# Two feed-forward layers after a channel attention: the first layer's cosine taken unreduced in all blocks, with its weights' decoding re-ordered

## The chip, the core and the metric

The program runs on one core of a Trainium2 chip. The metric is the device time of one execution in microseconds (us). Three timed runs of the kernel before gave 997.1, 998.02 and 998.35 us; their median, 998.02 us, is the time that the change is measured against.

## What is computed

With q, k, v of 6016 tokens by 256 channels, q and k are normalised per channel over the tokens, and

```
s = kn.T @ qn / tau            # 256 x 256
a = softmax(s)
x = v @ a                      # 6016 x 256
h = x @ w_in1                  # 256 -> 2048
y = (h * cos(h)) @ w_out1      # 2048 -> 256
out = silu-gated layer 2 of y: (g * sigmoid(g)) @ w_out2 with g = y @ w_in2
```

All four weight matrices come as 64-bit floats and are decoded to 32-bit floats on the core.

## The kernel before

**Stages.** First the q/k tiles are streamed in and the scores s are summed on TensorE; then the softmax; then `a` is folded into w_in1 (a times w_in1), so that the first layer reads v directly; then both layers, with tokens in 12 blocks (eleven of 512, one of 384). TensorE works in 32-bit products split in a high and a low part, three products for one (high*high, low*high, high*low: `PASSES`).

**The stretch that the change touches** runs from the end of the scores to the end of blocks 0, 1 and 2 of the first layer. It is a loop over 24 units (`units`, at the end of `direct`, lines 1103 to 1213). A unit is one block and one pair of 128 hidden columns; units 0 to 15 are blocks 0 and 1 (two units of one, two of the other, in turn), units 16 to 23 block 2. Units 0 to 3 need the first quarter of the folded w_in1, units 4 to 7 the second, and so on. In turn i the loop issues:

- TensorE: `emit_h`, twelve matmuls that make h of unit i in a PSUM room (line 742; two rooms alternate, `next_room`).
- units 0 to 15 only, `emit_first`: ScalarE rounds h/2pi + 1/4 to a whole number (line 749), VectorE subtracts that many times 2pi (line 750). Then `emit_cos`: ScalarE's sine (757) and VectorE's product with h (758), which frees the room. From unit 16 on `cosine_in` (1099) takes the sine of h itself with a scale per block: `small[b]` is 1 where a bound on |h| is at most 1.5 and 0 where it isn't (one 0 makes the program run a general path behind its end).
- `emit_split` of unit i-1: ScalarE writes the high part (763), VectorE the low part (764).
- TensorE: `emit_o1` of unit i-2, twelve matmuls with w_out1 (line 777).

**What rides along.** Strings of short names say what else is issued where; `steps_of` runs them, and each engine works in the order in which things were issued. `BEFORE` comes between softmax and unit 0; `EARLY` has the turns: `ahead` (before h), `amid` (after h), `inner` (after the split), `outer` (after the cosine). For a piece of w_in1 (W) or w_out1 (O), of which there are four each:

- `lW`, `l`: load (SyncE's queue; four raw buffers in a ring).
- `bW`, `bO` (`begin`): ScalarE's absolute value (336), and GpSimd's rounding of the low words (290; `aO`, `aW` put that on ScalarE).
- `cW`, `cO` (`clamp`): VectorE's clamp (295) and shift (303).
- `jW`, `jO` (`join`): VectorE joins sign and word (309), then GpSimd adds the low word (312).
- `sO` (`split`): ScalarE's high part (355), GpSimd's low part (356).
- `f00`, `f01`, `f10`, `f11`, `f2`, `f3` (`fold`): TensorE's matmuls of a quarter or half quarter of w_in1 (672) and ScalarE's high part of it (680). `l00` to `l31` (`fold_low`): VectorE's low part (688). Quarter j of the fold reads piece j of w_in1 after its `jW`.
- `lv`, `s1`, `v1`, `s0`, `v0`: load, high and low part of v's blocks 1 and 0 (401, 452, 455). One raw buffer for v: the next load waits until the last one was read.
- `tb`: a load of ScalarE's table.

`SPANS` places VectorE's maxima of the folded w_in1 (`span_of_weights`, 418); the bounds for blocks 2 and 3 (`bound`, 435 to 440) are made in turns 15 and 22. `FORMING` places work for blocks after these.

Of the kernel before, what the change touches and what calls it, by code (L numbers as in the profile page):

```python
# [53 lines left out]
WARM = (5, 0)  # L54

FRONT = {14: 'lW aW', 15: 'cW', 17: 'jW'}
AFTER = 'lW V l aW lW l cW'
THEN = ['', '', 'lW jW s0', '']
SIDE = [7, 11, 15, 20]
JOINED = 22  # L60
BEFORE = 'aO T0 T1 bW rs f00 v0 cO l00 lv tb f01 l01 cW jO f10 aO l l10'
TURNS = 16
FORMING = {
    12: 'A0', 13: 'A1', 15: 'B0', 16: 'B1', 17: 'V', 18: 'V', 19: 'V A2', 20: 'A3', 21: 'B2', 22: 'B3'
}
# [154 lines left out]
def direct(ctx, tc, qk, vT, tau, w_in1, w_out1, w_in2, w_out2, outT, dp, kept, within):  # L220
# [177 lines left out]
    def load_v(b):  # L398
        t0, n = BLOCKS[b]
        raw = io.tile([P, CH, TB], F32, tag="vraw", name=f"vraw{b}", bufs=1)  # L400
        nc.sync.dma_start(out=raw[:, :, :n], in_=vT.rearrange("(a p) n -> p a n", p=P)[:, :, t0 : t0 + n])
        return raw

    def span_of(b, raw, a=None):
# [9 lines left out]
            apply_absolute_value=True,  # L414
        )

    def span_of_weights(j, a):
        nc.vector.tensor_reduce(
            out=largest[:, j, a : a + 1],
            in_=fold_to(j, a, 0).bitcast(F32),  # L420
            axis=AX.XY,
            op=ALU.max,
            apply_absolute_value=True,
        )
# [16 lines left out]
            out=small[b], in0=most_of_all, scalar1=LIMIT, scalar2=1.0, op0=ALU.is_le, op1=ALU.mult  # L441
        )

    def split_v(b, raw, pool=False):
        n = BLOCKS[b][1]
        hi, lo = xparts[1, b] = [x_tile(s, b) for s in ("hi", "lo")]
        if pool:
            nc.gpsimd.tensor_scalar(
                out=halves(hi[:, :, :n]), in0=turns(raw[:, :, :n]), scalar1=1.0, scalar2=1.0, op0=ALU.mult, op1=ALU.mult
            )  # L450
        else:
            nc.scalar.activation(halves(hi[:, :, :n]), turns(raw[:, :, :n]), AF.Copy)

        def low():
            (nc.gpsimd if pool else nc.vector).tensor_tensor(
                out=halves(lo[:, :, :n]), in0=turns(raw[:, :, :n]), in1=halves(hi[:, :, :n]).bitcast(F32), op=ALU.subtract
            )

        return low
# [36 lines left out]
    calls = {
        "V": lambda: vraw0.append(load_v(0)),
        "s0": lambda: low_v0.append(split_v(0, vraw0.pop())),
        "v0": lambda: low_v0.pop()(),
        "lv": lambda: vraw1.append(load_v(1)),  # L500
        "s1": lambda: low_v1.append(split_v(1, vraw1.pop())),
        "v1": lambda: low_v1.pop()(),
        "p1": lambda: split_v(1, vraw1.pop(), pool=True)(),
        "l": WO1.load,
        "lW": W1.load,
        "bW": W1.begin,
# [151 lines left out]
    def next_room():  # L658
        turn_of[0] += 1
        return ps_hs[(turn_of[0] - 1) % 2]  # L660

    pws = {}

    def fold(j, a):
        if j < 2 or a == 0:
            pool, tag = (ps_o, "o") if j == 1 else (next_room(), "h")
            pw = pool.tile([P, CH, TB], F32, tag=tag, name=f"pw{j}{a}")
            pws.update({(j, i): pw[:, i] for i in ((a,) if j < 2 else range(CH))})
        halves_ = (a,) if j < 2 else range(CH)
        for a in halves_:  # L670
            for d in range(CH):
                nc.tensor.matmul(  # L672
                    pws[j, a],
                    ET[:, d, a * P : (a + 1) * P],
                    w1[:, d, j * TB : (j + 1) * TB],
                    start=(d == 0),
                    stop=(d == CH - 1),
                )
        for a in halves_:
            nc.scalar.activation(  # L680
                fold_to(j, a, 0), pws[j, a].rearrange("p (m f) -> p m f", m=2), AF.Copy, scale=rs[:, a : a + 1]
            )

    def fold_to(j, a, i):
        return wa[j][:, i].rearrange("p m (a f) -> p a m f", a=CH)[:, a]
# [48 lines left out]
    def emit_h(u):  # L734
# [10 lines left out]
    def emit_first(i, u, hp):  # L745
        n = BLOCKS[u[0]][1]
        t = flat(T[i % 2])
        k = t.bitcast(I32)[:, :, :n]
        nc.scalar.activation(k, hp[:, :, :n], AF.Copy, scale=1.0 / TWO_PI, bias=0.25)
        nc.vector.scalar_tensor_tensor(  # L750
            out=t[:, :, :n], in0=k, scalar=-TWO_PI, in1=hp[:, :, :n], op0=ALU.mult, op1=ALU.add
        )
        return t

    def emit_cos(u, hp, t):
        n = BLOCKS[u[0]][1]
        nc.scalar.activation(t[:, :, :n], t[:, :, :n], AF.Sin, bias=half_pi)
        nc.vector.tensor_tensor(out=t[:, :, :n], in0=hp[:, :, :n], in1=t[:, :, :n], op=ALU.mult)
# [349 lines left out]
    vs = []  # L1108
    for i, u in enumerate(units):
        b, m = u  # L1110
        steps_of(EARLY["ahead"].get(i, ""))
        if i == TURNS - 1:
            pro.close()
            rp = ctx.enter_context(tc.tile_pool(name="rp", bufs=1))
# [8 lines left out]
        if bounded is not None:  # L1123
            emit_o1(units[i - LAG], parts[i - LAG], (0,))
            if bounded == FIRST:
                ready.append(h_tile(f"bound{bounded}"))
                bound(bounded, ready[0][:, 1])
            else:
                bound(bounded, o1_room(bounded)[:, 0])
# [6 lines left out]
        if i < TURNS:  # L1136
            emit_cos(u, hp, t)
        else:
            cosine_in(b, hp, flat(T[i % 2]))
        pend = i  # L1140
        steps_of(EARLY["outer"].get(i, ""))
        if i >= TURNS:
# [296 lines left out]
    def tail_of_first(j):  # L1439
        nonlocal q_sums, late  # L1440
        _, b, m = slots[j]
        aside(b, m)
        behind(b, m)
        if m == 2:
            load_x2(0)
        if m == 4:
            p1_room.close()
            sp = ctx.enter_context(tc.tile_pool(name="sp", bufs=1, side="right"))
            q_sums = sp.tile([P, NU, HB], F32, name="q")
            late = [sp.tile([P, NU, HB], F32R, name=f"late{k}") for k in range(2)]  # L1450
            nc.vector.tensor_reduce(out=every, in_=smalls[:, FIRST:], axis=AX.X, op=ALU.min)
# [153 lines left out]
```

## Time and profile before

| | |
|---|---|
| median of three runs | 998.02 us (997.1 to 998.35) |
| the profiled execution | 998.62 us, of which its span (first to last instruction) is 996.8 us |
| TensorE busy | 983.0 us, 99% of the span |
| VectorE, ScalarE, GpSimd busy | 839.8, 792.9, 402.6 us |
| granted TensorE clock | 0.999 of full speed over the span |

The busy time of TensorE is from matmuls whose ends are modelled, so a small wait can hide in it; how far TensorE gets is better read from the start times of its groups of twelve matmuls. Times in the rows are us from the span's start; PE is TensorE, PEld its weight load, DVE VectorE, ACT ScalarE, POOL GpSimd, SPq SyncE's queue, L764 line 764.

### The profile page before, as it was taken

How to read it: one execution, taken by the hardware profiler on the slowest of the kernel's cores; microseconds unless marked ns; L12 is line 12 of the kernel's file. 1: busy time of each engine (PE TensorE's matmuls, PEld its weight loads, DVE VectorE, ACT ScalarE, POOL GpSimd, SP SyncE). 2: the span in 40 equal slices, each digit the busy share in tenths (PEclk: the TensorE clock that was granted, in tenths of full speed). 3: DMA queues.
4: the chain of work that ended last, by engine and by line, in shares of the span. 5: the costliest groups of instructions: out<-in, count | busy, mean ns of one | idle time of the engine just before them, and what ended most of it. 6: DMA issues, size and time to landing. Idle time of an engine off the chain costs nothing.

```text
span 996.8 us, 18691 instructions
## 1 busy us (share of the span) xinstructions
PE 983.0 (99%) x7062; PEld 927.6 (93%) x7062; DVE 839.8 (84%) x1287; ACT 792.9 (80%) x1453; POOL 402.6 (40%) x383
## 2 busy tenths in 40 slices
PE   9999999999999999999999999999999999999997
PEld 8867888899999999999999999999999999999997
DVE  5789898988878787888874889999999999999972
ACT  6786667688888888888876888888888888888863
POOL 4443277848678677686463111111111111111100
PEclk9999999999999999999999999999999999999999
DMA  9931005813434333334479722022022022121001
GB/s 339 382 125 51 1 4 240 321 59 127 159 127 159 138 127 137 138 133 149 179 278 383 308 104 84 25 85 72 36 85 75 33 86 67 41 86 49 33 12 40
DMA packets 35011, 126.58 MB, mean 127 GB/s; under 512 B 3170, under 2 KB 4450, under 8 KB 30178
## 3 DMA queue, kind: packets, MB, share of 16 engines
q1 hardware_dynamic: 34770, 125.12, 34.1%
q8 instruction: 57, 0.93, 0.4%
q14 instruction: 40, 0.33, 0.1%
q10 hardware_dynamic: 144, 0.20, 0.1%
HBM read 73.01 MB, written 52.30 MB: 126 GB/s over the span
## 4 chain that ended last, share of the span: by engine, by line
PE 87%; DVE 7%; ACT 2%; issue 2%; DMA 2%; POOL 0%; SPq 0%; DVEq 0%; ACTq 0%
PE o L991 20%; PE xz L991 20%; PE o L1343 16%; PE ys L991 15%; PE o L777 5%; PE h L742 3%; PE o L1031 2%; DMA qk<-qk_dram 2%; PE S L547 1%; DVE lo L764 1%; PE pw L672 1%; PE xz L1020 1%; PE ys L1020 1%; PE xz L1298 1%; PE ys L1298 1%
## 5 line engine op out<-in xcount | busy, mean ns | idle before, releaser
L807 DVE TENSOR_TENSOR lo<-t,hi 128x768 fp32r<-128x768 f32 (+1 forms) x176 | 194.9, 1117 | 28.9 <-ACT hi L799 28.8
L794 POOL TENSOR_TENSOR t<-t 128x256 f32<-128x256 f32 x88 | 64.4, 732 | 356.8 <-DVE t L791 296.8
L799 ACT ACTIVATE hi<-t 128x768 fp32r<-128x768 f32 (+1 forms) x176 | 168.9, 960 | 27.0 <-PE o L991 26.4
L1343 PE MATMUL o<-hi,wo 128*128 128x512 f32 x512 | 142.0, 380 | 0.0
L991 PE MATMUL o<-hi,wo 128*128 128x256 f32 x770 | 134.7, 275 | 0.0
L991 PEld LDWEIGHTS o<-hi,wo 128*128 128x128 f32 x770 | 117.1, 192 | 0.0
L991 PE MATMUL o<-lo,wo 128*128 128x256 f32 x385 | 105.9, 275 | 0.0
L1343 PEld LDWEIGHTS o<-hi,wo 128*128 128x128 f32 x512 | 87.4, 191 | 6.8
L1397 DVE TENSOR_TENSOR xz<-xz,t 128x512 f32<-128x512 f32 x64 | 44.7, 698 | 41.1 <-ACT t L1391 40.1
L1343 PE MATMUL o<-lo,wo 128*128 128x512 f32 x256 | 76.2, 380 | 0.0
L991 PEld LDWEIGHTS ys<-xhi,wf 128*128 128x128 f32 x384 | 67.8, 190 | 8.1 <-DVE ys L1041 1.0
L991 PE MATMUL ys<-xhi,wf 128*128 128x256 f32 x384 | 74.3, 275 | 1.0 <-DVE ys L1041 0.8
L991 PEld LDWEIGHTS o<-lo,wo 128*128 128x128 f32 x385 | 74.0, 192 | 0.0
L991 PE MATMUL xz<-xhi,wa 128*128 128x256 f32 x384 | 71.9, 276 | 0.0
L1501 ACT ACTIVATE ys<-xz 128x256 f32<-128x256 f32 x88 | 32.4, 368 | 45.8 <-PE xz L991 44.8
L991 PEld LDWEIGHTS xz<-xhi,wa 128*128 128x128 f32 x384 | 62.9, 191 | 3.4
L991 PE MATMUL xz<-x2hi,wf 128*128 128x256 f32 x352 | 65.8, 275 | 0.0
L991 PE MATMUL xz<-x2hi,wa 128*128 128x256 f32 x352 | 65.8, 275 | 0.0
L777 PE MATMUL o<-hi,wo 128*128 128x512 f32 (+1 forms) x256 | 62.5, 367 | 0.0
L786 DVE TENSOR_TENSOR t<-t 128x512 f32<-128x512 f32 x88 | 60.3, 685 | 0.1
L1531 ACT ACTIVATE t<-t 128x512 f32<-128x512 f32 x88 | 55.6, 632 | 2.3 <-DVE t L1041 2.1
L1388 ACT ACTIVATE ys<-xz 128x256 f32<-128x256 f32 x64 | 23.6, 368 | 38.9 <-PE xz L991 38.9
(268 smaller groups left out, 3186.7 us busy)
## 6 DMA issues: line engine op xcount, KB each, us to landing
qk<-qk_dram SPq DMA_DIRECT2D x22, 512.0 KB, 7.6
x2hi<-xshi SPq DMA_DIRECT2D x11, 896.0 KB, 5.3
x2lo<-xslo SPq DMA_DIRECT2D x11, 896.0 KB, 7.1
wi_dram<-stage SPq DMA_DIRECT2D x8, 1024.0 KB, 3.9
wo_dram<-stage SPq DMA_DIRECT2D x8, 1024.0 KB, 4.1
vraw<-vT_dram SPq DMA_DIRECT2D x11, 512.0 KB, 4.0
outT_dram<-q SPq DMA_DIRECT2D x22, 256.0 KB, 2.0
xshi<-t SPq DMA_DIRECT2D x10, 512.0 KB, 5.3
```

The costliest lines, as they stand in the source:

```text
L742: nc.tensor.matmul(hp[:, s, :n], lhsT, rhs, start=(i == 0), stop=(i == len(todo) - 1))
L777: nc.tensor.matmul(o[:, e, :n], wo1_at(i, f)[:, e * P : (e + 1) * P], columns(parts[k][:, s, :n]), start=(f == 0 and (i, k) == PASSES[0]), ...
L786: eng.tensor_tensor(out=t[:, 4:6, :c], in0=t[:, 0:1, :c].to_broadcast([P, 2, c]), in1=t[:, 1:3, :c], op=ALU.subtract)
L794: eng.tensor_tensor(out=t[:, 7, :c], in0=t[:, 3, :c], in1=t[:, 6, :c], op=ALU.subtract)
L799: nc.scalar.activation(hi[:, sl, :c], t[:, 1:][:, sl, :c], AF.Copy)
L807: nc.vector.tensor_tensor(out=lo[:, sl, :c], in0=t[:, 1:][:, sl, :c], in1=hi[:, sl, :c].bitcast(F32), op=ALU.subtract)
L991: nc.tensor.matmul(out, w(p, ka), columns(x[r][:, kb - 1]), start=(start and i == 0), stop=(stop and i == 2), skip_group_check=True,)
L1343: nc.tensor.matmul(o[:, e], wo1_at(i, f)[:, e * P : (e + 1) * P], columns(parts[k][:, s]), start=(f == 0 and (i, k) == PASSES[0]), stop=(f ...
L1388: nc.scalar.activation(y2, x2, AF.Copy)
L1397: nc.vector.tensor_tensor(out=xz[k], in0=xz[k], in1=sines[:, 1], op=ALU.mult)
L1501: nc.scalar.activation(y2, x2, AF.Copy)
L1531: nc.scalar.activation(t[:, 0:2], t[:, 0:2], AF.Silu)
```

## The change

Units 0 to 15 take their cosine as block 2 does: `emit_first` and `emit_cos` go, `cosine_in` is called for all 24. Its scale for blocks 0 and 1 comes from a bound per block and quarter of w_in1 (`bound_piece`): two small matmuls of the quarter's column maxima (`largest`) with the maxima of the block (`firsts`), a maximum and a comparison on VectorE, and the sine waits for that comparison. For the first quarter this is done in turn 0 (block 0) and turn 2 (block 1), for the others in turns 4, 8 and 12 for both blocks at once; there the bound's matmuls stand between the two halves of `emit_o1`.

The order of what rides along is new. w_out1's piece 0, not w_in1's piece 1, is decoded during the scores. Only the first quarter is folded before unit 0. Fold 1 stands in turn 3, fold 2 in turn 6 and fold 3 in turn 10, each between the turn's h and its o (`amid`); their high parts (`e1`, `e2`, `e3`), low parts and maxima (`w10`, `w11`, ...) follow in `outer`. w_in1's piece 2 is clamped and joined in the `outer` of turn 5, piece 3 clamped in that of turn 8 and joined in that of turn 9. Block 0's low part (`v0`) goes from VectorE to GpSimd; `x0` and `x1` are VectorE's maxima of blocks 0 and 1.

```diff
-AFTER = 'lW V l aW lW l cW'
-THEN = ['', '', 'lW jW s0', '']
+AFTER = 'l V lW aO l lW cO'
+THEN = ['', '', 'jO s0', '']
-BEFORE = 'aO T0 T1 bW rs f00 v0 cO l00 lv tb f01 l01 cW jO f10 aO l l10'
+BEFORE = 'v0 sO T0 T1 bW rs f00 x0 lv l00 f01 w00 l01 w01 tb x1 s1 l'
-SPANS = {1: (0, 0), 3: (0, 1), 5: (1, 0), 7: (1, 1), 9: (2, 0), 11: (2, 1), 12: (3, 0), 13: (3, 1)}
-EARLY = {'ahead': {2: 'f11', 3: 'cO', 6: 'f2 l21 l20', 10: 'f3 l31 l30'}, 'amid': {3: 'bW'}, 'inner': {0: 's1 v1', 1: 'jW', 2: 'l11', 6: 'cO', 11: 'jO'}, 'outer': {0: 'sO', 3: 'jO', 4: 'sO', 5: 'cW jW bO', 7: 'jO', 9: 'l sO bO', 10: 'cO', 12: 'sO'}}
+EARLY = {
+    'amid': {3: 'f1', 6: 'f2', 10: 'f3'},
+    'mid': {0: 'v1'},
+    'outer': {
+        0: 'cW', 1: 'bO jW', 2: 'cO lW', 3: 'e1 l10 l11 bW w10 w11', 4: 'jO', 5: 'cW jW sO l',
+        6: 'e2 l20 l21 bO w20 w21', 7: 'cO jO bW', 8: 'cW sO', 9: 'jW',
+        10: 'e3 l30 l31 bO w30 w31', 11: 'cO jO', 12: 'sO',
+    },
+}
...
+    def bound_piece(j, bs, room):
+        n = len(bs)
+        to, most_of_all = room[:, : n * TB // P], room[:, P : P + n]
+        for a in range(CH):
+            nc.tensor.matmul(
+                to,
+                largest[:, j, a : a + 1].to_broadcast([P, P]),
+                firsts[:, a, bs[0] : bs[-1] + 1].rearrange("p b j -> p (b j)"),
...
+        nc.vector.tensor_reduce(out=most_of_all, in_=to.rearrange("p (b j) -> p b j", b=n), axis=AX.X, op=ALU.max)
+        nc.vector.tensor_scalar(
...
+        "v0": lambda: low_v.pop(0)(nc.gpsimd),
+        "x0": lambda: span_of_first(0, raw_v.pop(0)),
+        "x1": lambda: span_of_first(1, raw_v[1]),
...
+    def cosine_in(i, h):
+        b, m = units[i]
+        out = flat(T[i % 2])
+        j = m // 2 * FIRST + b
+        nc.scalar.activation(out, h, AF.Sin, bias=half_pi, scale=smalls[:, j : j + 1] if b < FIRST else small[b])
+        steps_of(EARLY["mid"].get(i, ""))
         nc.vector.tensor_tensor(out=out, in0=h, in1=out, op=ALU.mult)
...
         hp = emit_h(u)
-        bounded = {TURNS - 1: FIRST, TURNS + 6: FIRST + 1}.get(i)
+        bounded = i in (4, 8, 12, TURNS - 1, TURNS + 6)
+        if bounded:
             emit_o1(units[i - LAG], parts[i - LAG], (0,))
-        if i < TURNS:
-            t = emit_first(i, u, hp)
+        if i in (0, 2):
+            bound_piece(0, (b,), o1_room(b)[:, 0])
         steps_of(EARLY["amid"].get(i, ""))
         if pend is not None:
             parts[pend] = emit_split(pend, units[pend])
-        steps_of(EARLY["inner"].get(i, ""))
+        if i == TURNS + 6:
+            bound(FIRST + 1, o1_room(FIRST + 1)[:, 0])
+        elif bounded:
+            ready.append(h_tile(f"bound{i}"))
+            if i < TURNS - 1:
+                bound_piece(i // 4, range(FIRST), ready[0][:, 1])
+            else:
+                bound(FIRST, ready[0][:, 1])
+        cosine_in(i, hp)
         pend = i
         steps_of(EARLY["outer"].get(i, ""))
```

At the end of the kernel the smallest of all the comparisons, now 18 columns and not 10, decides on the fallback.

## Rows read from the trace of the kernel before

**Rows 1.** The page: busy time of each engine, its share of the span, instructions.
```profile
PE 983.0 (99%) x7062; PEld 927.6 (93%) x7062; DVE 839.8 (84%) x1287; ACT 792.9 (80%) x1453; POOL 402.6 (40%) x383
```

**Rows 2.** TensorE's waits, 45 to 200 us: us in total, times, longest.
```profile
PE o L777 <- DVE lo L764: 1.7, 3, 0.9
...
PE h L742 <- DVE t L758: 1.2, 1, 1.2
...
PE bound L742 <- DVE smalls L440: 0.6, 1, 0.6
```

**Rows 3.** The last chain in order of time, 80 to 148 us: start, us, what.
```profile
88.45 3.43 PE pw L672 x8
91.88 2.59 PE h L742 x12
```

**Rows 4.** TensorE's timeline: first fold, h of unit 4, o of units 8, 14.
```profile
51.28 5.32 PE L672 MATMUL pw<-w,ET 128*128 128x512 f32 x12
...
76.63 1.10 PE L742 MATMUL h<-xhi,wa 128*128 128x512 f32 x4
...
118.54 1.03 PE L777 MATMUL o<-hi,wo 128*128 128x512 f32 x4
...
150.63 1.03 PE L777 MATMUL o<-hi,wo 128*128 128x512 f32 x4
```

**Rows 5.** Groups, 51 to 190 us: busy us, mean ns | idle before, releaser.
```profile
L750 DVE SCALAR_TENSOR_TENSOR t<-t,h 128x1024 f32<-128x1024 int32 x16 | 19.5, 1220 | 2.2 <-ACT t L749 2.1
L758 DVE TENSOR_TENSOR t<-h,t 128x1024 f32<-128x1024 f32 x16 | 19.5, 1217 | 0.4
...
L749 ACT ACTIVATE t<-h 128x1024 int32<-128x1024 f32 x16 | 16.4, 1025 | 12.5 <-PE h L742 10.3 <-DVE lo L764 2.1
...
L1100 ACT ACTIVATE t<-h,half_pi,smalls 128x1024 f32<-128x1024 f32 x6 | 7.2, 1200 | 1.1 <-PE h L742 1.1
...
L688 DVE SCALAR_TENSOR_TENSOR wa<-pw,rs,wa 128x512 fp32r<-128x512 f32 x8 | 5.8, 749 | 2.8 <-ACT wa L680 2.8
...
L680 ACT ACTIVATE wa<-pw,rs 128x512 fp32r<-128x512 f32 x8 | 5.1, 677 | 0.9 <-PE pw L672 0.9
...
L290 POOL TENSOR_SCALAR raw_wo<-raw_wo 128x1024 int32<-128x1024 uint32 x2 | 3.2, 1604 | 0.2
```

**Rows 6.** VectorE's and GpSimd's timelines, 91 to 95 us: a decode.
```profile
91.29 0.68 DVE L295 TENSOR_SCALAR w<-w 128x1024 f32<-128x1024 f32 x1
92.00 0.69 DVE L303 TENSOR_SCALAR w<-w 128x1024 int32<-128x1024 int32 x1
92.73 1.50 DVE L309 SCALAR_TENSOR_TENSOR w<-raw_w,w 128x1024 int32<-128x1024 int32 x1
94.15 0.67 DVE L418 TENSOR_REDUCE largest<-wa 128x1 f32<-128x512 f32 x1
...
94.31 2.43 POOL L312 TENSOR_TENSOR w<-w,raw_w 128x1024 int32<-128x1024 int32 x1 [5.16 <-DVE w L309]
```

**Rows 7.** VectorE's and GpSimd's timelines, 136 to 142 and 173 to 177 us.
```profile
136.47 2.04 DVE L764 TENSOR_TENSOR lo<-t,hi 128x1024 fp32r<-128x1024 f32 x1
...
139.57 1.21 DVE L409 TENSOR_REDUCE most<-vraw 128x8 bf16<-128x1024 f32 x1
...
136.15 3.50 POOL L957 TENSOR_TENSOR w1base<-wa 128x512 f32<-128x512 f32 x2
139.73 1.43 POOL L965 TENSOR_TENSOR w1form<-w1base 128x256 f32<-128x256 f32 x2
...
173.00 1.21 DVE L862 TENSOR_TENSOR t<-y,t 128x1024 fp32r<-128x1024 f32 x1
...
173.16 3.32 POOL L965 TENSOR_TENSOR w1form<-w1base 128x256 f32<-128x256 f32 x2 [0.63 <-DVE w1base L957]
```

**Rows 8.** VectorE's maximum for a bound; landing of v's block 1, issued at 53 us.
```profile
147.47 0.16 DVE L439 TENSOR_REDUCE bound<-bound 128x1 f32<-128x4 f32 x1
...
DMA to landing us min/median/max: 4.0/4.0/4.0
```

More of the change, by code (lines that the diff above doesn't have):

```diff
@@ L48 @@
 GROUPS = [1, 1] + 22 * [2] + [1]
+FIRST = 2
 LATE = 4
@@ L248, in direct @@
     most = {}
-    largest = wp.tile([P, 4, CH], F32, name="largest")
+    largest = wp.tile([P, 4, CH], BF16, name="largest")
     widest = wp.tile([P, CH], BF16, name="widest")
     every = wp.tile([P, 1], F32, name="every")
-    smalls = wp.tile([P, NB], F32, name="smalls")
-    small = {b: smalls[:, b : b + 1] for b in range(NB)}
+    smalls = wp.tile([P, 4 * FIRST + NB - FIRST], F32, name="smalls")
+    small = {b: smalls[:, 3 * FIRST + b : 3 * FIRST + b + 1] for b in range(FIRST, NB)}
+    firsts = wp.tile([P, CH, FIRST, TB // P], BF16, name="firsts")
     class Weights:
@@ L415, in span_of, with span_of_first @@
         )
+    def span_of_first(b, raw):
+        nc.vector.tensor_reduce(
+            out=firsts[:, :, b],
+            in_=raw.rearrange("p a (j n) -> p a j n", n=P),
+            axis=AX.X,
+            op=ALU.max,
+            apply_absolute_value=True,
+        )
+    def bound_piece(j, bs, room):
[6 more added lines that the diff above has]
+                firsts[:, a, bs[0] : bs[-1] + 1].rearrange("p b j -> p (b j)"),
+                start=(a == 0),
+                stop=(a == CH - 1),
+            )
+        nc.vector.tensor_reduce(out=most_of_all, in_=to.rearrange("p (b j) -> p b j", b=n), axis=AX.X, op=ALU.max)
+        nc.vector.tensor_scalar(
+            out=smalls[:, FIRST * j + bs[0] : FIRST * j + bs[-1] + 1],
+            in0=most_of_all,
+            scalar1=LIMIT,
+            scalar2=1.0,
+            op0=ALU.is_le,
+            op1=ALU.mult,
+        )
     def span_of_weights(j, a):
@@ L442, in bound, with split_v, low @@
         )
-    def split_v(b, raw, pool=False):
+    def split_v(b, raw):
         n = BLOCKS[b][1]
         hi, lo = xparts[1, b] = [x_tile(s, b) for s in ("hi", "lo")]
[L447 to L455, printed above, removed]
+        nc.scalar.activation(halves(hi[:, :, :n]), turns(raw[:, :, :n]), AF.Copy)
+        def low(eng=nc.vector):
+            eng.tensor_tensor(
                 out=halves(lo[:, :, :n]), in0=turns(raw[:, :, :n]), in1=halves(hi[:, :, :n]).bitcast(F32), op=ALU.subtract
@@ L493, in direct @@
     )
-    vraw0, vraw1, low_v0, low_v1 = [], [], [], []
+    raw_v, low_v = {}, {}
     calls = {
[L497 to L503, printed above, removed]
+        "V": lambda: raw_v.update({0: load_v(0)}),
+        "s0": lambda: low_v.update({0: split_v(0, raw_v[0])}),
+        "v0": lambda: low_v.pop(0)(nc.gpsimd),
+        "x0": lambda: span_of_first(0, raw_v.pop(0)),
+        "lv": lambda: raw_v.update({1: load_v(1)}),
+        "x1": lambda: span_of_first(1, raw_v[1]),
+        "s1": lambda: low_v.update({1: split_v(1, raw_v.pop(1))}),
+        "v1": lambda: low_v.pop(1)(),
         "l": WO1.load,
@@ L662, in direct, with fold_room, fold_high, fold_half @@
     pws = {}
+    def fold_room(j, halves_):
+        pw = next_room().tile([P, CH, TB], F32, tag="h", name=f"pw{j}{halves_[0]}")
+        pws.update({(j, i): pw[:, i] for i in halves_})
     def fold(j, a):
[L665 to L681, printed above, removed]
-            )
+        for d in range(CH):
+            nc.tensor.matmul(
+                pws[j, a],
+                ET[:, d, a * P : (a + 1) * P],
+                w1[:, d, j * TB : (j + 1) * TB],
+                start=(d == 0),
+                stop=(d == CH - 1),
+            )
+    def fold_high(j, a):
+        nc.scalar.activation(
+            fold_to(j, a, 0), pws[j, a].rearrange("p (m f) -> p m f", m=2), AF.Copy, scale=rs[:, a : a + 1]
+        )
+    def fold_half(a):
+        fold_room(0, (a,))
+        fold(0, a)
+        fold_high(0, a)
+    def fold_whole(j):
+        fold_room(j, range(CH))
+        for a in range(CH):
+            fold(j, a)
+    def fold_highs(j):
+        for a in range(CH):
+            fold_high(j, a)
     def fold_to(j, a, i):
@@ L697, in direct @@
     for j in range(NF // 4):
-        calls[f"f{j}"] = lambda j=j: fold(j, 0)
+        calls[f"f{j}"] = lambda j=j: fold_whole(j)
+        calls[f"e{j}"] = lambda j=j: fold_highs(j)
         for a in range(CH):
-            calls[f"f{j}{a}"] = lambda j=j, a=a: fold(j, a)
+            calls[f"f0{a}"] = lambda a=a: fold_half(a)
             calls[f"l{j}{a}"] = lambda j=j, a=a: fold_low(j, a)
+            calls[f"w{j}{a}"] = lambda j=j, a=a: span_of_weights(j, a)
     steps_of(BEFORE)
@@ L743, in emit_h @@
         return hp
[L745 to L758, printed above, removed]
     def emit_split(i, u):
@@ L1110, in direct @@
         b, m = u
-        steps_of(EARLY["ahead"].get(i, ""))
         if i == TURNS - 1:
@@ L1121, in direct @@
         hp = emit_h(u)
-        bounded = {TURNS - 1: FIRST, TURNS + 6: FIRST + 1}.get(i)
-        if bounded is not None:
+        bounded = i in (4, 8, 12, TURNS - 1, TURNS + 6)
+        if bounded:
             emit_o1(units[i - LAG], parts[i - LAG], (0,))
[L1125 to L1129, printed above, removed]
-        if i < TURNS:
-            t = emit_first(i, u, hp)
+        if i in (0, 2):
+            bound_piece(0, (b,), o1_room(b)[:, 0])
         steps_of(EARLY["amid"].get(i, ""))
@@ L1134, in direct @@
             parts[pend] = emit_split(pend, units[pend])
-        steps_of(EARLY["inner"].get(i, ""))
[L1136 to L1139, printed above, removed]
+        if i == TURNS + 6:
[7 more added lines that the diff above has]
+        cosine_in(i, hp)
         pend = i
@@ L1155, in direct @@
             vraw = load_v(FIRST + 1)
-        if i in SPANS:
-            span_of_weights(*SPANS[i])
         for what in FORMING.get(i, "").split():
@@ L1173, in direct @@
             v = units[i - LAG]
-            emit_o1(v, parts.pop(i - LAG), (0, 1) if bounded is None else (1,))
+            emit_o1(v, parts.pop(i - LAG), (1,) if bounded else (0, 1))
             if v[1] == NPAIR - 1:
@@ L1450, in tail_of_first @@
             late = [sp.tile([P, NU, HB], F32R, name=f"late{k}") for k in range(2)]
-            nc.vector.tensor_reduce(out=every, in_=smalls[:, FIRST:], axis=AX.X, op=ALU.min)
+            nc.vector.tensor_reduce(out=every, in_=smalls, axis=AX.X, op=ALU.min)
             nc.vector.tensor_copy(within, every[0:1])
```

3 lines of the change are left out of this document (removed).

## Prediction

> **What bounds the kernel now.** The busy row comes first: TensorE is busy 99% of the span, the next engine 84% [rows 1]. A wait of TensorE is therefore lost for good, and work taken off another engine counts only where TensorE waits for it. So the second view is who waited for whom in the stretch that is changed: three waits for a low part (1.7 us), one of h for its room (1.2 us), one for a bound (0.6 us) [rows 2]. The third is the chain, for the price of TensorE's own work: 2.59 us for twelve matmuls of h or o, 3.43 us for a whole fold [rows 3]. With these prices TensorE's start times tell what is lost [rows 4]. From h of unit 4 (76.63) to o of unit 8 (118.54) are 41.9 us; thirteen groups and two folds are 13 x 2.59 + 2 x 3.43 = 40.5; lost: 1.4. From there to o of unit 14 (150.63) are 32.1 us for twelve groups, 31.1; lost: 1.0. More than what is lost up to here and before unit 4 can't be won.
>
> The fourth view is the one that decides: VectorE's and GpSimd's operations side by side. A low part (two inputs in SBUF) takes 2.04 us beside GpSimd's operations, while a like operation before which nothing runs takes 1.21 [rows 7]. The pair of GpSimd's operations at 136.15 ends at 139.65, and 3.50 is just 1.2 + 1.1 + 1.2: one of GpSimd's, the low part, the other one. At 173 GpSimd was released by VectorE, but VectorE's next operation had begun 0.16 us earlier and took its plain 1.21; GpSimd's pair took 3.32 where it takes 1.43 alone [rows 7]. So **these operations run one after the other, each whole**, and at a hand-over VectorE's next one is first: it starts a little before the last one ends (94.15 against 92.73 + 1.50), GpSimd's add at 94.31 [rows 6]. A reduction with one input keeps 1.21 beside GpSimd [rows 7], and so does the product, which reads PSUM.
>
> **What goes.** ScalarE's rounding, 16 of 1.03 us, and VectorE's subtraction, 16 of 1.22 us [rows 5]. Both lie beside TensorE's 5.2 us per unit; the waits for a low part and a room are what they cost. I take all of those waits from unit 4 to unit 14 as gone.
>
> **What comes, up to unit 4.** I take 1.2 for the sine [rows 5], 1.14 for a product or low part (1.22 less the 0.08 that neighbours overlap), and start to start 0.7 for clamp and for shift, 1.42 for the sign step, 2.4 for GpSimd's add [rows 6]. A bound costs TensorE between 0 and two full matmuls (2.59 / 6 = 0.43); its two have a few columns, so I take 0.1. Its maximum and comparison take 0.4 with their hand-overs [rows 8].
> - From 51.28: two half folds to 54.7; the second half's high part 0.7 to 55.4 and low part 0.75 to 56.15 [rows 5]; nine of h's twelve matmuls remain: 58.1. Bound to 58.6, sine 59.8, product 61.0. TensorE ends h of unit 1 at 60.8, so h of unit 2 waits 0.2 for its room. The two maxima x0, x1 (1.21 each, like the row at 139.57) fit before the bound; x1 is queued ahead of the bound's maximum and waits for block 1, which if it lands 4.0 after 53.4 [rows 8] costs 0.4 more; fewer loads are ahead of it now, so I take 0.
> - From 61.0 VectorE does clamp, shift, low part 0, product 1 (to 64.7), the sign step of w_in1's piece 1 (66.1) and block 1's bound (66.5). GpSimd's add came first meanwhile and holds low part 1 back to 68.6; that ends at 69.7, product 2 at 70.85. Fold 1 needs the room that product 2 frees, and TensorE is there at 61.0 + 3 x 2.59 + 0.1 = 68.9: it **waits 1.95**. After fold and o, h of unit 4 starts at 76.9, against 76.63: +0.3.
>
> Three moves I cost at 0. v0 on GpSimd (2.4) lies beside both half folds and the wait for their high parts; without that cover its overrun would show. The loads moved on SyncE's queue have three turns and more (over 15 us) to their decode, with nothing urgent behind them; one that is late costs at most its landing, some 4 [rows 8]. The swapped pieces have the same size, so softmax starts as before.
>
> **Fold 2.** Zero is the end of h of unit 4. Half of o 1.3, bound 1.4, compared 1.8, sine 3.0, product 4.15, sign step of w_out1's piece 1 (turn 4) 5.6, low part 4 first, 6.7; GpSimd's add runs 6.7 to 9.1; product 5 at 7.85. Now turn 5's clamp of w_in1's piece 2 stands in VectorE's queue: does it wait for the add? No row shows a clamp beside GpSimd. From below: it doesn't (0.7, like the one-input reduction); from above: it waits for all of GpSimd's operation. I take the upper value: at 0.68 us for 1024 columns [rows 6] it reads as fast as an operation with two inputs, twice as fast as the reduction. So clamp 9.8, shift 10.5, sign step 11.95, low part 5 first 13.1, add 15.5. Fold 2 reads that piece, and TensorE is there at 5.3 (h of unit 5) + 2.59 + 2.59 = 10.5: it **waits 5.0**. Behind it stands o of unit 4, and everything after.
>
> The Trainium skill, page "SBUF — State Buffer", section "Who interferes with whom", says that a tensor_scalar can run in a mode that uses both of VectorE's port pairs, and then VectorE and GpSimd exclude each other for a whole instruction. No run shows this yet for clamp and shift; by it the total below stands, without it the first rival's does.
>
> **Fold 3.** Zero is the end of h of unit 8. Product 7 was at -2.85; clamp, shift and sign step of w_out1's piece 2 to 0, low part 7 to 1.15, GpSimd's add to 3.55, its rounding of w_in1's piece 3 (1.6 [rows 5]) to 5.15. Product 8 is at 4.15, the clamp of piece 3 waits to 5.15 and ends at 5.85; GpSimd's low part of w_out1 (2.4, as the add) to 8.25; shift 9.0, low part 8 10.1, product 9 11.25, sign step 12.7, low part 9 13.8, add 16.2. TensorE is there at 10.5: it **waits 5.7**.
>
> **Sum.** To unit 4: +0.3. To o of unit 8: +5.0 + 5.7 + 0.2 (two bounds) - 1.4 = +9.5. To o of unit 14: 1.0 lost before, 0.2 now (two bounds): -0.8. Behind that the order is the same, and TensorE hides the rest: 0. Together +9.0. The profiled execution took 998.62 us, its span 996.8 and 1.8 around it; +9.0 gives 1007.6. It was 0.6 above the median of 998.02, so the forecast for the median is **1007.0 us**.
>
> **The rivals.**
> - *Clamp and shift don't wait for GpSimd.* Fold 2: clamp and shift to 9.3, add done at 14.25, wait 3.75. Fold 3: low part 8 waits for GpSimd's to 7.55, add done at 14.8, wait 4.3. That is 2.65 less: 1004.4. For it: no row shows the opposite. Chance 0.20.
> - *GpSimd's add is first after the sign step.* It would end 1.1 earlier in both folds: 1004.7; with the first rival too 1002.1. The row at 173.16 speaks against it. Chance 0.15.
> - *Nothing waits for the other engine.* Then fold 1 doesn't wait (-1.95), fold 2 waits 2.6 (add done at 13.1), fold 3 1.2: 998.2, no change. The row of 2.04 us speaks against it; for it, that GpSimd is free for long stretches. Chance 0.10.
> - *The decode is done before the fold asks*, and the relief of VectorE remains: no fold waits, so 9.0 - 1.95 - 5.0 - 5.7 = -3.65: 994.4, faster. It decides from the point where the add is done within 5.2 us of the end of the h before (that of unit 5, of unit 9); with the two waits under 1.6 us together the kernel is faster by over 2 us. Against it: sine, product, sign step and add alone are 1.2 + 1.14 + 1.42 + 2.4 = 6.2. Chance 0.05.
> - That the bounds fail and the general path runs too is no case of its own: those of blocks 2 to 11 take maxima over all quarters, these over one.
>
> **How the numbers follow.** The forecast has 0.50. The range goes from 1002.0, where the first two rivals meet, to 1009.5: block 1 landing late 0.4, and up to half a microsecond for VectorE being late at each of the four bounds from turn 4 on. Below lie the last two rivals with 0.15. A measurement of this kernel tells about 0.2%, 2 us, from no change. All cases but the last two are slower by more: 0.85; within: 0.10; faster: 0.05.
>
> **What would show it.** In the profile after, TensorE's waits should name fold 2 and fold 3 (line of the fold's matmuls) behind GpSimd's add of w_in1, about 5 us each, and fold 1 behind the product, about 2. GpSimd's add should show 3.5 us behind a sign step, and the clamp of piece 2 and shift of piece 3 well over 0.7. The three waits for low parts between units 4 and 14 should be gone. If the folds start within a microsecond of the end of the h before them, I am wrong; if they wait 2.6 and 1.2, it is the exclusion that isn't there.

## The result and the profile after

The changed kernel takes **1011.7 us** (median of 4 runs, 1010.8 to 1012.5) against 998.1 for the kernel before (997.1 to 998.4, now with a fourth run): ratio 1.014, 95% interval 1.012 to 1.0155. It is slower by 13.6 us where 9.0 were forecast; 1011.7 lies above the range (1002.0 to 1009.5). The profiled execution took 1012.3 us, its span 1010.4, so 13.6 more span than the 996.8 of before.

The busy row, which answers to [rows 1]:
```profile
PE 987.2 (98%) x7072; PEld 929.4 (92%) x7072; DVE 826.5 (82%) x1282; ACT 778.0 (77%) x1435; POOL 412.4 (41%) x386
```
VectorE is busy 13.3 us less and ScalarE 14.9 less, as the change set out to do. But TensorE is busy 4.2 us *more* (983.0 before), though it got only a few tiny matmuls for the bounds. A matmul that is busy for longer without more work is the first sign of the part that the prediction didn't have.

TensorE's waits, 45 to 210 us (total, times, longest), which answer to [rows 2]:
```profile
PE pw L705 <- POOL w L321: 9.7, 2, 5.1
PE pw L705 <- DVE t L1140: 1.7, 1, 1.7
...
PE h L792 <- DVE t L1140: 1.1, 1, 1.1
PE o L812 <- DVE lo L799: 0.8, 1, 0.8
```
Two folds (line 705) wait 9.7 us together for GpSimd's add of w_in1 (line 321); fold 1 waits for a product. No wait for a low part is left up to o of unit 14; the one of 0.8 us stands at 207 us. TensorE's timeline, which answers to [rows 4], shows where and how long each is:
```profile
50.91 3.60 PE L705 MATMUL pw<-w,ET 128*128 128x512 f32 x8
...
62.24 1.10 PE L792 MATMUL h<-xhi,wa 128*128 128x512 f32 x4 [1.15 <-DVE t L1140]
...
72.05 3.67 PE L705 MATMUL pw<-w,ET 128*128 128x512 f32 x8 [1.65 <-DVE t L1140]
...
96.02 6.47 PE L705 MATMUL pw<-w,ET 128*128 128x512 f32 x8 [4.61 <-POOL w L321]
...
128.49 5.60 PE L705 MATMUL pw<-w,ET 128*128 128x512 f32 x8 [5.13 <-POOL w L321]
...
165.30 1.03 PE L812 MATMUL o<-hi,wo 128*128 128x512 f32 x4
```
Folds 2 and 3 wait 4.61 and 5.13 us, and then the same eight matmuls take 6.47 and 5.60 us, where the chain of before has a fold at 3.43 [rows 3] and fold 1 here has 3.67. That is 3.04 + 2.17 = **5.2 us that stand in no wait**. The table of stretches tells where most of them come from: the row holds the stretch, its length, busy us of TensorE, its weight loads, VectorE, ScalarE and GpSimd, then the granted clock.
```profile
91.20:96.00 4.80, 0.21 (x1) 0.00 (x0) 3.62 (x4) 1.97 (x2) 3.27 (x2) 0.87 0.91 318
96.00:98.00 2.00, 1.98 (x3) 0.95 (x4) 0.00 (x0) 0.00 (x0) 2.00 (x1) 0.50 0.04 14
98.00:100.00 2.00, 2.00 (x4) 0.90 (x3) 0.00 (x0) 0.00 (x0) 1.43 (x2) 0.50 0.00 0
100.00:102.00 2.00, 2.00 (x5) 0.78 (x3) 0.00 (x0) 0.00 (x0) 0.00 (x0) 0.60 0.00 0
102.00:104.00 2.00, 2.00 (x10) 1.57 (x9) 0.18 (x1) 1.48 (x3) 0.00 (x0) 1.00 0.00 0
```
During this wait the granted clock begins to fall (0.87 over the whole wait), and through most of the fold it is 0.50, the lower of its two levels (1.2 GHz): three to five matmuls in 2 us, where from 102 us on, at 2.4 GHz again, there are ten. Fold 3 shows the same (0.50 from 128.4 to 132). So these two folds ran most of their length at half speed; fold 1, which had waited 1.65 us, ran at full speed.

The chain of waits from fold 1's end to fold 2 (start, us, what), which answers to [rows 3]:
```profile
82.28 0.18 DVE bound L446
...
82.76 1.22 ACT t L1138
...
85.14 1.50 DVE wv_wo L318
86.64 1.13 DVE lo L799
87.77 1.14 DVE t L1140
88.91 1.70 DVE w L304
90.63 0.70 DVE w L312
...
91.36 1.24 DVE w L318
...
92.73 3.24 POOL w L321
...
96.02 6.47 PE pw L705 x8
```
This is the queue of the prediction, piece by piece: bound, sine, product, sign step of w_out1, low part 4, product 5, clamp, shift, sign step, add. VectorE and GpSimd side by side, which answers to [rows 6]:
```profile
88.83 1.77 DVE L304 TENSOR_SCALAR w<-w 128x1024 f32<-128x1024 f32 x1
...
92.50 1.22 DVE L799 TENSOR_TENSOR lo<-t,hi 128x1024 fp32r<-128x1024 f32 x1
```
```profile
86.79 3.24 POOL L321 TENSOR_TENSOR wv_wo<-wv_wo,raw_wo 128x1024 int32<-128x1024 int32 x1 [15.06 <-DVE wv_wo L318]
92.73 3.23 POOL L321 TENSOR_TENSOR w<-w,raw_w 128x1024 int32<-128x1024 int32 x1 [2.69 <-DVE w L318]
```
The clamp, 0.68 us alone [rows 6], takes 1.77: it ends 0.57 us after GpSimd's first add does (90.03), which is about its own length. The add takes 3.2 us instead of 2.43, since low part 5 began 0.23 us ahead of it. Ahead of fold 3 the shift of piece 3 shows the same against GpSimd's low part of w_out1:
```profile
118.74 2.78 DVE L312 TENSOR_SCALAR w<-w 128x1024 int32<-128x1024 int32 x1
```

The account in stretches, as the lead of the kernel before. At h of unit 4 it is 1.5 us (78.14 against 76.63). O of unit 8 is read from the chain of both profiles, since in the timeline the modelled end of the slow fold overlaps it; the first row is after, the second before:
```profile
134.08 2.59 PE o L812 x12
```
```profile
118.70 2.59 PE o L777 x12
```
That is a lead of 15.4, 13.9 more: 9.7 of waits and 5.2 of slow folds, less 1.1 for the relief net of the bounds. At o of unit 14 it is 14.7 (165.30 against 150.63), 0.7 less. Behind that it shrinks by another 1.1, to 13.6.

### The profile page after: what moved, and what is told of

It reads as the page before. It is cut to its first block, busy times and chain, and to the rows that moved or that the text cites. A ratio compares the mean times of both kernels' runs of the same rounds, so it can differ in the third digit from the quotient of the medians.

```text
span 1010.4 us, 18715 instructions
## 1 busy us (share of the span) xinstructions
PE 987.2 (98%) x7072; PEld 929.4 (92%) x7072; DVE 826.5 (82%) x1282; ACT 778.0 (77%) x1435; POOL 412.4 (41%) x386
## 4 chain that ended last, share of the span: by engine, by line
PE 83%; DVE 8%; POOL 3%; issue 2%; DMA 2%; ACT 1%; SPq 0%; DVEq 0%; POOLq 0%; ACTq 0%
PE o L1026 20%; PE xz L1026 20%; PE o L1377 16%; PE ys L1026 15%; PE o L812 3%; DVE lo L799 2%; PE pw L705 2%; PE o L1066 2%; DMA qk<-qk_dram 2%; DVE t L1140 1%; PE S L582 1%; PE h L792 1%; POOL w1form L1000 1%; PE xz L1055 1%; PE ys L1055 1%
## 5 line engine op out<-in xcount | busy, mean ns | idle before, releaser
L1535 ACT ACTIVATE ys<-xz 128x256 f32<-128x256 f32 x88 | 32.4, 368 | 45.8 <-PE xz L1026 44.8
L1026 PE MATMUL o<-hi,late 128*128 128x256 f32 x308 | 53.8, 275 | 0.0
```

Source lines behind the costliest of these rows:

```text
L1026: nc.tensor.matmul(out, w(p, ka), columns(x[r][:, kb - 1]), start=(start and i == 0), stop=(stop and i == 2), skip_group_check=True,)
L1535: nc.scalar.activation(y2, x2, AF.Copy)
```

## The experiments

The ratios are to the kernel before, timed on the same chip. Differences to the changed kernel's 1011.7 us are between medians of a few runs from different sessions, between which the kernel before moved by 0.8 us (997.4 to 998.2).

**The clock by itself.** Ahead of folds 2 and 3 TensorE gets matmuls to do whose result is overwritten by the fold:
```
 def fold_whole(j):
     fold_room(j, range(CH))
+    for _ in range({2: 20, 3: 23}.get(j, 0)):
+        nc.tensor.matmul(
+            pws[j, 0], wo1_at(0, 0)[:, :P], wo1[0][:, 0, 0, :TB], start=True, stop=True, skip_group_check=True
+        )
     for a in range(CH):
         fold(j, a)
```


> The changed kernel with idle matmuls put ahead of folds 2 and 3 (20 and 23 products of 128x128 by 128x512, whose result the fold overwrites), so that TensorE works through its two waits. Theory (the waits of 4.6 and 5.1 us let the granted clock fall, and the folds behind them run at half of it): both folds take 3.4 us again, not 6.5 and 5.6, the granted clock stays at 1.0, and the time falls by 3.0 + 2.2 = 5.2, to about 1006.5 us; the folds still start when GpSimd's add is done. Rival (the folds are slow for what they read, a piece that GpSimd has just written): folds as slow as before, 1011.7 us or more.

Measured: 1008.5 us, ratio 1.011 (1.010 to 1.013), span 1006.8. The folds took 3.70 and 3.59 us and the clock stayed at 1.00 through both waits and both folds; the rival, which blames what the folds read, falls. The time is 2.0 above the 1006.5 that was expected. Part of that is that the 23 matmuls ahead of fold 3 held it until 126.38, 0.7 us beyond the end of the decode (125.69). So 20 in both places were tried:

> The run that filled the waits ahead of folds 2 and 3 with idle matmuls, with 20 instead of 23 of them ahead of fold 3, since the 23 ran 0.75 us beyond the decode's end. Theory (the clock's fall behind a wait costs 5.2 us, of which the first such run got back 4.4 and lost 0.75 to its own excess): both folds at 3.4 to 3.8 us, fold 3 starts within 0.2 us of its data, and the time is 0.5 to 0.8 us below that run's 1008.5, 1007.7 to 1008.1, ratio to the kernel before 1.0097 to 1.0105. Rival (with fewer of them the clock falls again ahead of fold 3): fold 3 takes over 5 us and the time is over 1009.

Measured: 1007.7 us, ratio 1.0096 (1.0081 to 1.0112); the profiled execution took 1007.1. TensorE's timeline of this run:
```profile
90.52 4.73 PE L726 MATMUL pw<-wo 128*128 128x512 f32 x20
95.34 3.70 PE L705 MATMUL pw<-w,ET 128*128 128x512 f32 x8
120.38 4.83 PE L726 MATMUL pw<-wo 128*128 128x512 f32 x20 [0.47 <-DVE t L1144]
125.10 3.70 PE L705 MATMUL pw<-w,ET 128*128 128x512 f32 x8
```
The decode is no faster, and the folds start when it ends, as before; only TensorE is kept at work. That alone gives back 4.0 us of the median and 5.2 of the span, of which 1.0 is the first fold's earlier start (49.92 against 50.91). The two folds are 2.77 + 1.90 = 4.7 us shorter. So of the 5.2 us above 4.7 are the clock's, a cost of its own on top of the wait; the other 0.5 is that a fold which starts afresh takes 3.70 at the upper clock too, where one that follows at once on other matmuls adds 3.43.

**Who is first at the hand-over.** Two tiny reductions (two columns, their result is overwritten later) go behind the sign steps of w_in1's pieces 2 and 3: VectorE gets more to do, but its next operation after the sign step is now a reduction with one input, of the kind that kept its time beside GpSimd [rows 7].
```
-4: 'jO', 5: 'cW jW sO l',
+4: 'jO', 5: 'cW jW z sO l',
...
-8: 'cW sO', 9: 'jW',
+8: 'cW sO', 9: 'jW z',
...
+for _ in range(2):
+    nc.vector.tensor_reduce(out=every, in_=smalls[:, :2], axis=AX.X, op=ALU.min)
```


> The changed kernel with work added to VectorE: two tiny one-input reductions (0.2 us each) behind the sign steps of w_in1's pieces 2 and 3, in turns 5 and 9. Theory (VectorE and GpSimd exclude each other, and VectorE's next operation is first at a hand-over): with a reduction next, GpSimd's add starts at once, takes 2.4 and not 3.2 to 3.4 us, the low part behind it waits instead; the folds wait about 0.8 to 1.1 us less each, so 1009.5 to 1010 us, and less if the clock falls later for it. Rival (GpSimd's add is slow by itself or for memory traffic): the add stays at 3.2 to 3.4, the time at 1011.7 or up to 0.8 above.

Measured: 1008.7 us, ratio 1.011 (1.010 to 1.013): more work for VectorE, and less time (3.0 us in the median, 1.7 between the two profiled executions). VectorE's and GpSimd's timelines behind the sign step:
```profile
92.58 0.34 DVE L554 TENSOR_REDUCE every<-smalls 128x1 f32<-128x2 f32 x2
92.85 3.43 DVE L805 TENSOR_TENSOR lo<-t,hi 128x1024 fp32r<-128x1024 f32 x1
...
92.81 2.37 POOL L321 TENSOR_TENSOR w<-w,raw_w 128x1024 int32<-128x1024 int32 x1 [2.69 <-DVE every L554]
```
GpSimd's add begins 0.04 us ahead of the low part, and now it is the low part that takes 3.43 us and the add that takes its plain 2.37. The waits fell by 0.86 and 0.98, to 3.75 and 4.15; the folds still took 5.40 and 6.22 (granted clock 0.50 in the midst of both), so most of the clock's part stayed.

**Where in the queue the decode stands.** One run brings w_in1's piece 3 ahead of w_out1's piece in turns 8 and 9 (the second pair of lines below); a second run has this and does the same for piece 2 in turns 4 and 5 (both pairs):
```
-4: 'jO', 5: 'cW jW sO l',
+4: 'cW jW', 5: 'jO sO l',
...
-8: 'cW sO', 9: 'jW',
+8: 'cW jW', 9: 'sO',
```


> The changed kernel with only piece 3 of w_in1 joined earlier (turn 8 in place of 9, and w_out1's split in turn 9). Theory: fold 3's wait falls from 5.1 to under 1 us and its fold from 5.6 to 3.4; fold 2 stays at a wait of 4.6 and 6.5 us for the fold: -4.4 - 2.2 = -6.6, about 1005 us. Rival (the second wait follows from the first, whatever the order): fold 3 still waits over 3 us.

Measured: 1005.7 us, ratio 1.009 (1.007 to 1.011). Fold 3 waits 1.09 and takes 3.70; fold 2, untouched, waits 4.58 and takes 5.40.

> The changed kernel with the decode of w_in1's pieces 2 and 3 a turn earlier and ahead of w_out1's: clamp and join of piece 2 in turn 4 (w_out1's join from turn 4 to turn 5), clamp and join of piece 3 in turn 8 (w_out1's split from turn 8 to turn 9). Theory (the folds wait because their piece is joined in the turn just before): fold 2 doesn't wait, fold 3 under 1 us; o of unit 4 now waits some 3 to 4 us for w_out1's low part, which is late in place of it; no wait is long enough to bring the clock down for a whole fold. -4.6 - 5.1 - 5.2 + 3.7 + 0.7 = -10.5: about 1001 us. Rival (the folds wait for their PSUM room or for VectorE's lateness in general): both waits stay, within 2 us of 1011.7.

Measured: 1002.3 us, ratio 1.0056 (1.0035 to 1.0077). Fold 2 waits 0.19, fold 3 1.14, both take 3.70. Now o of unit 4 waits 1.77 for w_out1's low part, which was put behind. Both runs add up to within the noise. In the first, fold 3 loses 4.0 us of wait and 1.9 of slow clock, and the untouched fold 2 happens to take 1.1 less than in the changed kernel: 7.0 together, against 6.8 in the spans of the profiled executions (1003.6 against 1010.4) and 6.0 in the medians. In the second, fold 2 loses 4.4 and 1.7, and 2.7 come back (o of unit 4 waits 0.94 for w_out1's high part, too): 3.4 together, against 2.8 in the spans and 3.4 in the medians. Executions of one and the same kernel spread over 3 to 4 us here.

**The bounds.** The five bounds of blocks 0 and 1 go; ones stand as the scale, so the condition under which the unreduced cosine may be taken is left out for these blocks.

> The changed kernel without the five bounds of blocks 0 and 1 (their scale is a column of ones; the comparison that they stand for is left out). Theory (the place of the decode makes the waits, the bounds only lengthen the chain ahead of them): fold 1 waits 0.9 and not 1.65, fold 2 about 1.5 less than 4.6, fold 3 about as long as now; 1.0 for the bounds' matmuls and fold 1, 1.5 for fold 2: about 1009 us, some 2 less if the clock falls less in fold 2. Rival (it is the sine's wait for a bound that holds the folds up): both long waits go, 1000 us or less.

Measured: 1008.6 us, ratio 1.011 (1.009 to 1.012), near the 1009 that were forecast. Without the bounds (their maxima are still taken) folds 2 and 3 still wait, so the rival falls; the bounds are worth about 3 us of the 13.6. The rows of TensorE's timeline hold something else:
```profile
94.34 3.70 PE L706 MATMUL pw<-w,ET 128*128 128x512 f32 x8 [3.63 <-POOL w L321]
...
123.84 6.76 PE L706 MATMUL pw<-w,ET 128*128 128x512 f32 x8 [5.07 <-POOL w L321]
```
After 3.63 us of waiting the fold ran at the upper level throughout (1.00 in every stretch from 91 to 100), after 5.07 at the lower one (0.50 from 123.8 to 130).

**The relief by itself.** The kernel before, its order untouched, takes the sine of h of blocks 0 and 1 directly; again the bounds' condition is left out, with ones as the scale.
```
-if i < TURNS:
-    t = emit_first(i, u, hp)
...
-if i < TURNS:
-    emit_cos(u, hp, t)
-else:
-    cosine_in(b, hp, flat(T[i % 2]))
+cosine_in(b, hp, flat(T[i % 2]))
```


> The kernel before with its own order of the decode and folds, and only the reduction of h taken out: the sine of blocks 0 and 1 is taken of h itself, with a column of ones as scale (no bounds; the check that they stand for is left out). What the freed work of ScalarE and VectorE is worth by itself. Theory: only the waits for low parts between units 2 and 14 go, 2 to 3 us: 995 to 996 us. Rival (relief of VectorE, the second busiest engine, is worth more, or nothing): under 993, or 997.5 and more.

Measured: 993.1 us, ratio 0.9953 (0.9936 to 0.9969); span 992.6, 4.2 below before's. The gain is larger than the theory had it (995 to 996 us). In its trace the waits for low parts and for the bound are gone, and h of unit 2 still waits 1.1. TensorE's timeline:
```profile
147.16 1.03 PE L778 MATMUL o<-hi,wo 128*128 128x512 f32 x4
```
This is o of unit 14, 3.5 us earlier than before's 150.63 [rows 4], of which the first fold's earlier start is 0.3; the rest of the 4.2 comes behind it. The cosine without its reduction is worth about 4 to 5 us, and the order and the bounds that came with it cost 18.6 together.

**Bounds, but the old order.** The kernel before with the cosine of units 4 to 15 unreduced and bounded, units 0 to 3 as they were, the maxima of V in turns 2 and 3 and those of the folded w_in1 re-placed; nothing is left out.
```
+REDUCED = 4
...
-if i < TURNS:
+if i < REDUCED:
     t = emit_first(i, u, hp)
...
-3: 'jO', 4: 'sO',
+2: 'x0', 3: 'x1 jO', 4: 'sO',
...
+elif bounded:
+    ready.append(h_tile(f"bound{i}"))
+    if i < TURNS - 1:
+        bound_piece(i // 4, range(FIRST), ready[0][:, 1])
...
```


> The order of the kernel before with bounds: units 0 to 3 reduce h as before, units 4 to 15 take the sine unreduced by bounds for quarters 2 to 4, whose maxima are taken in turns 1 to 3, 6, 7, 10, 11 (the blocks' maxima from the high part of v, in turns 2 and 3). Nothing is left out. Theory (what the change can win is VectorE's relief, and the old order keeps it): the waits of units 0 to 3 stay as before, 1.5 to 2 us of the 5.0 that the old order won without bounds, and three bounds add 0.3 to 0.5: 994.5 to 995.5 us, under both kernels. Rival (the maxima and bounds eat the relief): 997 us or more.

Measured: 1003.5 us, ratio 1.006 (1.005 to 1.0075): a miss by 8 us. TensorE's timeline:
```profile
81.31 0.70 PE L812 MATMUL o<-lo,wo 128*128 128x512 f32 x2 [1.53 <-DVE lo L799]
83.74 0.20 PE L433 MATMUL bound<-firsts,largest 128*128 128x8 bf16 x2 [1.74 <-DVE firsts L421]
83.81 1.87 PE L812 MATMUL o<-hi,wo 128*128 128x512 f32 x4
...
113.22 1.13 PE L777 MATMUL bound<-xhi,wa 128*128 128x512 f32 x4 [1.73 <-DVE smalls L441]
```
VectorE has no idle time from 66 to 86 us; two maxima of 1.21 us put into its queue there make the low part late by 1.53 and the bound by 1.74. Those two waits stand close together, and the matmuls behind them are slow (1.87 instead of 1.03; granted clock 0.50 from 84 to 86). At 113 us the comparison, 0.16 us long, was queued behind a low part that GpSimd's add held for 3.13. The bound is cheap for TensorE (0.2 us for its two matmuls); its place on VectorE is not.

**Decode ahead.** The changed kernel, all of it, with the decodes spread a turn or more ahead of the fold that reads them and fold 3 one unit later:
```
-'amid': {3: 'f1', 6: 'f2', 10: 'f3'},
+'amid': {3: 'f1', 6: 'f2', 11: 'f3'},
...
-0: 'cW', 1: 'bO jW', 2: 'cO lW', 3: 'e1 l10 l11 bW w10 w11', 4: 'jO', 5: 'cW jW sO l',
-6: 'e2 l20 l21 bO w20 w21', 7: 'cO jO bW', 8: 'cW sO', 9: 'jW',
-10: 'e3 l30 l31 bO w30 w31', 11: 'cO jO', 12: 'sO',
+0: 'bO cW jW', 1: 'bW', 2: 'cW jW lW', 3: 'e1 l10 l11 cO w10 w11', 4: 'jO', 5: 'sO l',
+6: 'e2 l20 l21 bO bW cO w20 w21', 7: 'jO', 8: 'sO', 9: 'bO cW jW', 10: 'cO',
+11: 'e3 l30 l31 jO w30 w31', 13: 'sO',
```


> The changed kernel with a new order throughout: pieces 1 and 2 of w_in1 clamped and joined in turns 0 and 2, piece 3 in turn 9 with its fold in turn 11, w_out1's pieces in the turns between. Theory: no fold waits over 0.5 us, the clock stays up, and the relief of VectorE is left: about 2 us under the kernel before, 995 to 997 us. Rival (exclusion of VectorE and GpSimd makes any order with unreduced cosines and bounds lose): 999 us or more.

Measured: 996.1 us (10 runs), ratio 0.9981 (0.9971 to 0.9991): faster than both kernels, by 15.6 us than the changed one and by 0.2% than the one before, about as little as can be told. With the bounds kept, some 2 us are left of the 5 that the relief gave without them. TensorE's timeline and its waits, 45 to 200 us:
```profile
71.15 3.67 PE L705 MATMUL pw<-w,ET 128*128 128x512 f32 x8
...
90.35 3.60 PE L705 MATMUL pw<-w,ET 128*128 128x512 f32 x8
...
119.84 3.60 PE L705 MATMUL pw<-w,ET 128*128 128x512 f32 x8
```
```profile
PE h L792 <- DVE t L1140: 1.2, 1, 1.2
PE o L812 <- DVE lo L799: 0.9, 1, 0.9
```
No fold waits and none is slow. The largest wait left is that of h of unit 2. The next run goes after it, by putting block 1's maxima and its split of V behind the product of unit 0.

> The kernel of the run that decoded ahead of the folds, with block 1's maxima and its split of V moved from the start-up to behind the product of unit 0. There h of unit 2 waited 1.2 us for that product, which stood on VectorE behind the maxima. Theory (a wait of TensorE ahead of unit 4 is still worth its length at the end): h of unit 2 waits under 0.6 us, and the time is 0.4 to 0.7 us below that kernel's 996.1, 995.4 to 995.8. Rival (block 1's split, now later, is waited for by h of unit 2 in the product's place): 996.1 or more.

Measured: 998.1 us (11 runs), ratio 0.9997 (0.9988 to 1.0006). The rival held: h of unit 2 no longer waits for the product, but 0.41 for block 1's high part and 1.07 for its low part, and fold 1 starts 21.45 us after the first fold instead of 20.0.

**The two columns.** In the changed kernel the operation on the row sums (line 685, two columns, no matter in itself) takes 1.28 us:
```profile
51.45 1.28 DVE L685 TENSOR_SCALAR rs<-rs 128x2 f32<-128x2 f32 x1
```
GpSimd's low part of V runs from 50.28 to 52.70. In the last run that low part goes behind the row sums:
```
-BEFORE = 'v0 sO T0 T1 bW rs f00 x0 lv ...
+BEFORE = 'sO T0 T1 rs v0 bW f00 x0 lv ...
```


> The changed kernel with one move: GpSimd gets the low part of block 0's V behind the row sums of the first fold and behind w_out1's low part, not ahead of both, so that the two-column operation on the row sums finds no GpSimd instruction under way. Theory (that operation's 1.28 us is what made block 1 late): it takes under 0.3 us, the maxima of block 0 end and block 1's load is issued 0.9 to 1.1 us earlier (about 53.1), h of unit 2 starts 0.5 to 1.0 us earlier than 62.24, h of unit 4 likewise before 77.7, and the time is 0.5 to 1.0 us below the changed kernel's 1011.7, 1010.7 to 1011.2, if the later folds wait as long as they did. Rival (fold 2 asks that much earlier for the same decode, and waits that much longer): h of unit 4 is earlier but o of unit 8 is not, and the time stays at 1011.7. Second rival (the low part of V is now late for h of unit 0): TensorE waits there from about 56.2 on.

Measured: 1013.1 us, ratio 1.015 (1.014 to 1.017). This is no gain, and no clear loss either: the runs, 1011.6 to 1014.9, overlap those of the changed kernel. What holds the operation was right and the consequence was not: it takes 0.16 us, but block 1's load, counted from the first fold, is issued 2.3 us *later*, since it overwrites the V that the low part reads until 55.26, and h of unit 2 waits 3.21:
```profile
50.34 0.16 DVE L685 TENSOR_SCALAR rs<-rs 128x2 f32<-128x2 f32 x1
...
55.28 0.37 SPq L410 DMA_DIRECT2D vraw<-vT_dram  x1
```
```profile
63.25 2.05 PE L792 MATMUL h<-xhi,wa 128*128 128x512 f32 x4 [3.21 <-DVE t L1140]
```
Here too the matmuls behind the wait are slow, 2.05 instead of 1.10 us (granted clock 0.51 from 63.2 to 66).

## Why the prediction was too low

*Mechanism.* That of the waits held. The folds wait for GpSimd's add of w_in1, 4.61 and 5.13 us where 5.0 and 5.7 were worked out, and fold 1 waits 1.65 for the product where it was 1.95. The exclusion of clamp and shift, for which no row had stood, is now in the trace (1.77 and 2.78 us; even two columns took 1.28 beside GpSimd and 0.16 without it), so the first rival falls. The Trainium skill, page "SBUF — State Buffer", section "Who interferes with whom", has this exclusion, and adds that whoever issues first holds the ports for a whole instruction. These rows agree, and so does the run with the tiny reductions (add 2.37 us when it is first, 3.23 when the low part is). The second rival (the add is first after the sign step) falls by the adds of 3.2 and 3.4 us, and the run with the tiny reductions, which makes it true, shows its price: waits shorter by 1.84 where 2.3 had been worked out (1007.0 to 1004.7). One sign was misread: of the three waits for low parts [rows 2] only that of 0.9 stood between units 4 and 14; the others ended at 74.7 and 188.6 us, ahead of and behind that stretch.

*The step that failed* is the sum of the folds: it took a fold at 3.43 us whenever it started. The folds behind the two waits took 6.47 and 5.60, with the granted clock at 0.50 for most of their length: 5.2 us more, of which 4.7 are the clock's. No rival and no term of the range held this. The run with 20 idle matmuls in each wait shows it by itself: same decode, folds that start when it ends as before, 3.70 each, and 4.0 us less. With this term the forecast gives 1012.2. That this is so near to 1011.7 is in part luck, since the other misses cancel: 1.2 too little up to unit 4, 1.0 too much for the two waits, 1.1 of relief too little behind unit 14.

*Up to unit 4* the forecast had +0.3, and it was +1.5, with the first fold 0.4 earlier. The sentence that failed is the one that valued block 1's late landing at up to 0.4 and took 0. The row sums were held 1.1 us by GpSimd, so block 0's maxima and then block 1's load came late (issued 54.12, landed 57.9), and the bound's maximum stood behind block 1's maxima until 59.04; the sine began at 59.49, 0.9 later than the 58.6 worked out, in spite of the earlier first fold. It had been assumed that v0 on GpSimd lay wholly beside other work; a two-column operation was the work it did not lie beside. That the load also waits for that low part showed only when the low part was moved. So no run shows by itself what the hold cost; this part is argued from the chain.

*The relief* was sized right where it was looked for: from h of unit 4 to o of unit 8 it gave 1.1, net of the bounds, against 1.2, and from there to o of unit 14 0.7 against 0.8. It goes on behind unit 14, where 0 was taken and 1.1 came; what made up this 1.1 was not followed. In the old order it is worth 4.2 us of span.

*The fourth rival* (decode done before the fold asks, 994.4) is what the spread order made of the change: 996.1. Its condition was right, and the changed kernel's order just doesn't meet it.

## What to carry to other kernels

A wait of TensorE has two prices: its length, and the slow matmuls behind it. Here 9.7 us of waiting cost 5.2 more, 4.7 of it by the clock, so a forecast that finds a wait of some microseconds should be worked out with and without slow matmuls behind it. And when one engine is relieved, look at what its queue holds ahead of the next thing that TensorE asks for: here the place of the decode in the queue cost 15.6 us (what the run that decoded ahead got back), nearly four times the 4.2 that the relief gave in the old order.

## What was not expected of the hardware

- The granted clock's fall doesn't follow from the length of the wait alone. Behind waits of 3.21, 3.75, 4.15, 4.58, 4.61, 5.07, 5.13 and 5.14 us the next matmuls were slow; behind 3.63 they were not, and behind two short ones of 1.53 and 1.74 with little work between they were. What decides between them these runs do not settle. Nor does the fall always come in the wait: in the run with the tiny reductions the clock was 1.00 through the wait of 3.75 and fell with the fold under way (0.90 from 95.2 to 97, then 0.50). The slow folds took from 5.26 to 6.76 us.
- VectorE's next queued operation takes its turn ahead of a GpSimd operation that the last one releases, and two reductions of 0.17 us in between turn this round (add 3.23 against 2.37 us, low part 1.22 against 3.43).
- An operation of two columns can be held by GpSimd as one of 1024 is: 1.28 us instead of 0.16.
